# ScalarE's Sigmoid ahead of a nop, a difference behind a product, and a gate product one bundle earlier, in a fused convolution and channel-mix kernel

## The chip, the cores and the metric

The kernel runs on one core of a Trainium2 chip. Time is device time in microseconds (us) for one execution; a run's figure is the median of its executions. The engines of the core work side by side, each through its own queue in order: TensorE (PE in the profile, with PEld for its weight loads), VectorE (DVE), ScalarE (ACT), GpSimd (POOL) and SyncE (SP), of which the last here only issues transfers.

## The reference, cut to what matters

Eight sequences of 4160 rows with 192 columns go through a causal convolution over 7 rows, whose weights are a softmax for each of 8 heads, and then through a channel mix. `*` is elementwise, `@` a matrix product.

```python
# first stage: the convolution, per head h with 24 columns
out[b, s, h, :] = sum_k softmax(weight)[h, k] * x_padded[b, s + k, h, :]

# second stage, x is now the first stage's result
x_prev = x shifted by one row
xk = mu_k * x + (1 - mu_k) * x_prev
xr = mu_r * x + (1 - mu_r) * x_prev
k  = maximum(xk @ w_k, 0)            # 192 -> 1024 columns
v  = k * k @ w_v                     # 1024 -> 192 columns
r  = 1 / (1 + exp(-(xr @ w_r)))      # 192 -> 192 columns
out = r * v
```

## The kernel before

Sequences are worked on in pairs, p = 0 to 3, one in each half of the 128 partitions. A pair is cut into *steps* of 512 rows; the first pair begins and ends with a step of 256, and the last 64 rows of all pairs form one last step. Each step has `ns` slots (8 for 512 rows, 4 for 256): one slot is one tile of k, a product of six matmuls with 1024 results per partition. Four consecutive slots make a *bundle*. Bundles are counted from 0 (b0); step 8 is the second 256-row step of the first pair and fills b15, step 9 is the first of the second pair and fills b16 and b17. R and V are made in *quads* of 256 rows (s, j), one in each bundle, behind their step:

```python
quads = []
vb = 1
for s, (p, t0, L, n0, ns) in enumerate(steps):
    for j in range(L // 256):
        vb = max(vb, last_bundle[s]) + 1
        quads.append((s, j, vb))
```

All results of TensorE lie in one ring of four tiles[...]. k tiles, R tiles, V tiles and convolution tiles all come from it, and a tile's place is free again when the instruction that reads it out is done:

```python
ring = ctx.enter_context(tc.tile_pool(name="ring", bufs=4, space=bass.MemoryType.PSUM))

def k_relu(n):                                   # frees a k tile
    ...
    nc.scalar.activation(out=k_sb, in_=ps.rearrange("p a b -> p (a b)"), func=AF.Relu)

def r(s, j):                                     # twelve matmuls
    xr = xrs[s]
    ps = ring.tile([P, 2, BANK], FP32, tag="k", name="ps_r")
    ...

def r_out(s, j):                                 # frees an R tile
    r_sbs[s, j] = three.tile([P, 2, 2 * D], BF16, tag="r_sb", name="r_sb")
    nc.scalar.activation(out=r_sbs[s, j], in_=r_ps.pop((s, j))[:, :, 0 : 2 * D], func=AF.Sigmoid)

def v_rows(s, j, half, ks=(0, 1)):               # V, thirty-two matmuls in each half
    ...
    if half == 0:
        nc.scalar.clobber_nop([nc.scalar.lower_ap(v_ps[s, j])])

def v_out(s, j):                                 # V's product with R: frees a V tile
    ...
    nc.vector.tensor_tensor(out=..., in0=v_ps.pop((s, j)), in1=r_sbs.pop((s, j)), op=ALU.mult)
```

The nop is an instruction of ScalarE that does nothing. It waits for V's first half and V's second half waits for it, so that the two halves, which use the two row groups of TensorE with the two banks of the tile exchanged, never meet.

VectorE makes the inputs of k and R: a difference of two shifted views of the convolution's result, then `scale` by mu and `add_y` for xk and for xr. xk and xr have two buffers each, taken in turns by the steps:

```python
def diff(s, cs=slice(0, 3)):
    ...
    nc.vector.tensor_tensor(out=..., in0=y_of(s, cs, 1), in1=y_of(s, cs, 0), op=ALU.subtract)

def scale(s, i, *cs, act=False):
    ...
        (xks, xrs)[i][s] = two.tile([P, NC, STEP], BF16, tag=("xk", "xr")[i], name=("xk", "xr")[i])
    ...
```

The convolution of later rows is woven in as *units* of eight matmuls, two units in each of b2 to b5 and then in every odd bundle from b7 to b53; ScalarE copies each unit's tile out. Its result goes to memory and comes back by a transposing transfer (`y_read`), from which `diff` reads. From b3 on, all bundles with k tiles have this form, in the order in which each engine meets its share:

```python
def bundle_rest(b, ns):
    units = xt.get(b, [])
    quad = vq[b][0]
    for n in bundles[b - 1][2 if b == 3 else 3 :]:
        k_square(n)
    run(mix_a, b)
    if b > 3:
        v_out(*vq[b - 1][0])
    k_mm(ns[0])
    k_relu(ns[0])
    k_mm(ns[1])
    k_relu(ns[1])
    run(mix_b, b)
    k_square(ns[0])
    k_square(ns[1])
    run(mix_c, b)
    k_mm(ns[2])
    k_relu(ns[2])
    run(rq, b)            # r
    v_rows(*quad, 0)
    run(rs, b)            # r_out, the Sigmoid
    k_square(ns[2])
    k_mm(ns[3])
    k_relu(ns[3])
    for u in units:
        conv_tiles(*u)
        conv_tiles_out(*u)
    v_rows(*quad, 1)
    run(late, b)
```

What the tables hold of a step s whose first slots are in bundle fb:

```python
            if s == 2:
                at(mix_c, 1, diff, s)
            elif s == 4:
                at(mix_a, fb - 1, diff, s)
            else:
                at(mix_c, fb - 2, diff, s)
            at(mix_a, fb - 1, scale, s, 0, 0)
            at(mix_b, fb - 1, scale, s, 0, 1, 2)
            at(mix_c, fb - 1, add_y, s, 0)
            ...
                at(mix_c, fb - 1, scale, s, 1, 0)
                at(mix_a, fb, scale, s, 1, 1)
            at(mix_b, fb, scale, s, 1, 2)
            at(mix_b, fb, add_y, s, 1)
    ...
    for s, j, vb in quads:
        at(rq, vb - (s == LAST), r, s, j)
        at(rs, vb - (s == LAST), r_out, s, j)
        ...
```

Of the kernel before, what the change touches and what calls it, by code (L numbers as in the profile page):

```python
# [14 lines left out]
def kernel(  # L15
# [56 lines left out]
    T0, LAST = S - TAIL, len(steps) - 1  # L72
# [12 lines left out]
    last_bundle = [bundle_of[st[3] + st[4] - 1] for st in steps]  # L85
# [202 lines left out]
    def conv_tiles(g, c):  # L288

        nb = groups[g][2]  # L290
        if c == 0:
            ys[g] = two.tile([P, GB, 2 * D], BF16, tag="y", name="y")
        ps = ring.tile([P, 2, BANK], FP32, tag="k", name="ps_c")
        conv_ps[g, c] = ps
        m = nb // 2
        banks = ps[:, :, 0 : m * 4 * G].rearrange("p i (m s c) -> p i m s c", m=m, s=2)
        for k in range(2):
            h = 2 * c + k
            for i in range(2):
                q = slice(i * Q, (i + 1) * Q)  # L300
                for j in range(2):
                    nc.tensor.matmul(  # L302
                        out=banks[j * Q : (j + 1) * Q, i, :, :, k * G : (k + 1) * G],
                        lhsT=toe[q, h, q],
                        rhs=xbs[g][q, j * m : (j + 1) * m, :, h * G : (h + 1) * G],
                        start=True,
                        stop=True,
                    )
# [217 lines left out]
    def k_mm(n, cs=range(NC)):  # L526


        s, j = slots[n]
        L = steps[s][2]  # L530
        xk = xks[s]
        if cs[0] == 0 and n not in k_ps:
            k_ps[n] = ring.tile([P, 2, BANK], FP32, tag="k", name="ps_k")
        ps = k_ps[n]
        nf = STEP // L

        for c in cs:
            for f in range(nf):
                fs = slice((j * nf + f) * P, (j * nf + f + 1) * P)
                for i in range(2):  # L540
                    r = slice(i * Q, (i + 1) * Q)
                    nc.tensor.matmul(  # L542
                        out=ps[:, i, f * L : (f + 1) * L],
                        lhsT=wk[r, c, fs],
                        rhs=xk[r, c, :L],
                        start=c == 0 and f == 0,
                        stop=c == NC - 1 and f == nf - 1,
                    )

    def k_relu(n):  # L550
        ps = k_ps.pop(n)
        k_sb = four.tile([P, 2 * STEP], BF16, tag="k_sb", name="k_sb")
        k_sbs[n] = k_sb
        nc.scalar.activation(out=k_sb, in_=ps.rearrange("p a b -> p (a b)"), func=AF.Relu)  # L554

    def k_square(n):
        s, j = slots[n]
        L = steps[s][2]
        k_sb = k_sbs.pop(n)
        if j == 0:  # L560
            k2s[s] = three.tile([P, NF, 2 * STEP], BF16, tag="k2", name="k2")
        nf = STEP // L
        i = k_sb
        o = k2s[s][:, j, :]
        if nf > 1:
            i = k_sb.rearrange("p (b f t) -> p f b t", b=2, f=nf)
            o = k2s[s][:, j * nf : (j + 1) * nf, 0 : 2 * L].rearrange("p f (b t) -> p f b t", b=2)
        nc.vector.tensor_tensor(out=o, in0=i, in1=i, op=ALU.mult)  # L568
# [3 lines left out]
# [4 lines that stand above are left out]
# [44 lines left out]
    def v_rows(s, j, half, ks=(0, 1)):  # L620

        if half == 0:
            v_ps[s, j] = ring.tile([P, 2, BANK], FP32, tag="k", name="ps_v")[:, :, 0 : 2 * D]
        for k in ks:
            for f in range(NF):
                for i in range(2):
                    q = slice(i * Q, (i + 1) * Q)
                    bank = (i + half) % 2
                    t = tile_of(s, j, 2 * bank + k)
                    nc.tensor.matmul(  # L630
                        out=v_ps[s, j][:, bank, k * D : (k + 1) * D],
                        lhsT=k2s[s][q, f, t * P : (t + 1) * P],
                        rhs=wv[q, f, :],
                        start=half == 0 and k == 0 and f == 0,
                        stop=half == 1 and k == 1 and f == NF - 1,
                    )
        if half == 0:
            nc.scalar.clobber_nop([nc.scalar.lower_ap(v_ps[s, j])])

    def tile_of(s, j, k):  # L640
        return k // 2 * (steps[s][2] // P) + 2 * j + k % 2

    def v_out(s, j):
        p, t0, L, _, _ = steps[s]
        o_sb = three.tile([P, 4, D], FP32, tag="o_sb", name="o_sb")
        nc.vector.tensor_tensor(  # L646
            out=o_sb.rearrange("p (b t) d -> p b (t d)", b=2),
            in0=v_ps.pop((s, j)),
            in1=r_sbs.pop((s, j)),
            op=ALU.mult,  # L650
        )
        for st in range(2):
            c = t0 + 2 * j * P
            nc.sync.dma_start(
                out=out[2 * p + st, c : c + 2 * P, :].rearrange("(m p) d -> p m d", p=P),
                in_=o_sb[:, 2 * st : 2 * st + 2, :],
            )
# [24 lines left out]
    early, rq, rs, xt, mix_a, mix_b, mix_c, vq, late = ({} for _ in range(9))  # L682

    def at(table, b, fn, *a):
        table.setdefault(b, []).append((fn, a))
# [7 lines left out]
    for g, (p, base, nb, fb, on_pe) in enumerate(groups):  # L693
# [12 lines left out]
        if g > 4:  # L706

            b = {5: 1, 6: 2, 7: 7}.get(g)
            b = first_bundle[first_step[p]] + (-15, -11, -7, -3)[(g - 6) % 4] if b is None else b
# [3 lines left out]
    for s, (p, t0, L, n0, ns) in enumerate(steps):  # L713
        fb = first_bundle[s]
        if s == 0:
            at(mix_a, 1, mix, s, 1)
            continue
        if s == 1:
            at(mix_b, 1, scale, s, 1, 0, 1)
            at(late, 2, scale, s, 1, 2)  # L720
            at(late, 2, add_y, s, 1)
        else:
            if s == 2:
                at(mix_c, 1, diff, s)
            elif s == 4:
                at(mix_a, fb - 1, diff, s)
            else:
                at(mix_c, fb - 2, diff, s)
            at(mix_a, fb - 1, scale, s, 0, 0)
            at(mix_b, fb - 1, scale, s, 0, 1, 2)  # L730
            at(mix_c, fb - 1, add_y, s, 0)
            if s == 2:
                at(mix_a, fb, scale, s, 1, 0)
                at(mix_b, fb, scale, s, 1, 1)
# [5 lines that stand above are left out]
        if s == LAST - 1 or s < LAST and steps[s + 1][0] > p:  # L740
            at(late, fb - 1, keep_tail, p)
    for s, j, vb in quads:
        at(rq, vb - (s == LAST), r, s, j)
        at(rs, vb - (s == LAST), r_out, s, j)
        if s == LAST:
            at(late, vb, v_last, s, j)
        else:
            vq.setdefault(vb, []).append((s, j))

    def run(table, b):  # L750
        for fn, a in table.get(b, ()):
            fn(*a)
# [114 lines left out]
# [17 lines that stand above are left out]
        k_mm(ns[2])  # L884
        k_relu(ns[2])
        run(rq, b)
        v_rows(*quad, 0)
        run(rs, b)
        k_square(ns[2])
        k_mm(ns[3])  # L890
        k_relu(ns[3])
# [5 lines that stand above are left out]
# [87 lines left out]
```

## Time and profile before

| what | value |
|---|---|
| time, median of 3 | 424.53 us (424.3 to 425.72) |
| span of the profiled execution | 423.4 us, TensorE clock 0.999 of full |
| TensorE busy | 409.8 us (97%) |
| VectorE busy | 371.2 us (88%) |
| ScalarE busy | 354.9 us (84%) |
| V's matmuls, 4032 | 188.2 us |
| k's matmuls, 1632 | 190.8 us |
| R's matmuls, 780 | 43.2 us |
| convolution of later rows, 448 matmuls | 21.6 us |
| Relu of a k tile, 260 | 1032 ns each |
| Sigmoid, 65 | 811 ns each |
| V's product with R, 64 | 953 ns each |
| transfers | 65.58 MB, 155 GB/s in the mean |

Busy times of matmuls overlap, since two row groups of TensorE work side by side, so the shares of the lines add up to more than TensorE's. The clearest measure of pace is the distance from one bundle's R to the next one's: 5.73 us in a bundle without convolution and 6.57 us in one with two units of 240 columns, nearly everywhere from 53 us to the end.

In the lines below, L599 is R's matmuls, L610 the Sigmoid, L630 V's matmuls, L542 k's, L554 the Relu, L568 the square, L302 the convolution, L319 its copies, L480 `diff`, L516 `scale`, L522 `add_y` and L646 V's product. A line of the timeline gives start, length, engine, line, operation, tiles, shapes, count, and in brackets the idle time of the engine before it with what ended that time.

### The profile page before, as it was taken

To read this page: it belongs to the slowest core of one execution; us is meant where nothing else is said; L and a number is where in the kernel's file an instruction comes from. 1 tells how busy PE (TensorE), PEld (TensorE's weight loads), DVE (VectorE), ACT (ScalarE), POOL (GpSimd) and SP (SyncE) were. 2 spreads that over 40 slices of the span, in tenths; PEclk is the share of its full clock that TensorE was granted. 3 is DMA by queue.
4 is the path that set the end of the run, shared out by engine and by line. 5 is a ranking of instruction groups with operands and counts; after the bars stand their busy time and mean duration, and the time that the engine had idled before them with its cause. 6 is when DMAs were issued, how large, how long until landed. Compare 5 with 4: busy or idle time off the path is not lost.

```text
span 423.4 us, 16804 instructions
## 1 busy us (share of the span) xinstructions
PE 409.8 (97%) x7350; PEld 302.7 (71%) x7350; DVE 371.2 (88%) x671; ACT 354.9 (84%) x429; POOL 65.5 (15%) x102
## 2 busy tenths in 40 slices
PE   7899899999979999999999999999999999999996
PEld 5566576777757677677767677776777777777895
DVE  5989799999699889889989988898998889999973
ACT  6899978889768898888889888888898888877781
POOL 8650013012040110304022020302200000000000
PEclk9999999999999999999999999999999999999999
DMA  9999889979649696887859798696972735412223
GB/s 145 175 190 207 177 208 176 221 148 180 166 82 224 143 207 163 123 209 133 199 131 210 197 120 212 96 231 139 180 187 63 194 99 144 119 54 76 77 77 112
DMA packets 137657, 65.58 MB, mean 155 GB/s; under 512 B 87388, under 2 KB 137584, under 8 KB 137584
## 3 DMA queue, kind: packets, MB, share of 16 engines
q1 hardware_dynamic: 95840, 48.42, 43.1%
q0 software_dynamic: 40944, 15.53, 32.3%
q8 instruction: 57, 0.93, 0.9%
q10 hardware_dynamic: 800, 0.57, 0.4%
q14 instruction: 16, 0.13, 0.1%
HBM read 31.62 MB, written 37.09 MB: 162 GB/s over the span
## 4 chain that ended last, share of the span: by engine, by line
PE 86%; DMA 5%; DVE 3%; POOL 2%; issue 1%; ACT 1%; SPq 0%; DVEq 0%; ACTq 0%; POOLq 0%
PE ps_v L630 37%; PE ps_k L542 35%; PE ps_r L599 7%; PE ps_c L302 4%; DMA xb<-in_x_dram 2%; DMA yT<-y_dram 2%; PE ps_v L582 1%; DMA y_dram<-y 1%; POOL xb L136 1%; DVE k L568 1%; DVE o_sb L646 1%; POOL wk L208 1%; DVE xr L522 0%; DVE xr L516 0%; ACT y L319 0%
## 5 line engine op out<-in xcount | busy, mean ns | idle before, releaser
L554 ACT ACTIVATE k_sb<-ps_k 128x1024 bf16<-128x1024 f32 x260 | 252.8, 1032 | 30.5 <-PE ps_k L542 29.0
L568 DVE TENSOR_TENSOR k<-k_sb 128x1024 bf16<-128x1024 bf16 x260 | 173.0, 686 | 32.5 <-ACT k_sb L554 32.0
L542 PE MATMUL ps_k<-xk,wk 64*128 64x512 bf16 (+1 forms) x1632 | 190.8, 367 | 1.7 <-DVE xk L522 0.8
L630 PE MATMUL ps_v<-wv,k 64*128 64x192 bf16 x4032 | 188.2, 243 | 0.3 <-ACT k_sb L554 0.2
L630 PEld LDWEIGHTS <-k 64*128 64x128 bf16 x4032 | 168.0, 94 | 13.7 <-issue 4.5
L542 PEld LDWEIGHTS <-wk 64*128 64x128 bf16 x1632 | 80.4, 94 | 60.0 <-issue 2.1
L610 ACT ACTIVATE r_sb<-ps_r 128x768 bf16<-128x768 f32 x65 | 52.6, 811 | 25.0 <-PE ps_v L630 24.3
L136 POOL DMA_DIRECT2D xb<-in_x_dram x62 | 45.1, 734 | 180.3 <-issue 88.5
L646 DVE TENSOR_TENSOR o_sb<-ps_v,r_sb 128x768 f32<-128x768 f32 x64 | 61.0, 953 | 3.3 <-issue 2.4
L319 ACT CAST y<-ps_c 128x960 bf16<-128x960 f32 (+5 forms) x84 | 51.1, 698 | 0.0
L599 PEld LDWEIGHTS <-xr 64*128 64x128 bf16 x780 | 34.5, 94 | 19.7 <-issue 5.4
L599 PE MATMUL ps_r<-wr,xr 64*128 64x192 bf16 x780 | 43.2, 243 | 4.2 <-DVE o_sb L646 4.1
L516 DVE TENSOR_SCALAR xr<-d,mu 128x512 bf16<-128x512 bf16 (+1 forms) x102 | 35.1, 351 | 4.0 <-PE ps_r L599 4.0
L480 DVE TENSOR_TENSOR d<-yT 128x1536 bf16<-128x1536 bf16 (+3 forms) x37 | 31.4, 852 | 2.7 <-ACT yT L381 1.3
L516 DVE TENSOR_SCALAR xk<-d,mu 128x512 bf16<-128x512 bf16 (+1 forms) x98 | 31.9, 352 | 0.1
L522 DVE TENSOR_TENSOR xr<-xr,yT 128x1536 bf16<-128x1536 bf16 (+1 forms) x33 | 31.0, 939 | 1.1
L522 DVE TENSOR_TENSOR xk<-xk,yT 128x1536 bf16<-128x1536 bf16 (+2 forms) x34 | 30.5, 899 | 0.1
L302 PE MATMUL ps_c<-xb,toe 64*64 64x240 bf16 (+1 forms) x448 | 21.6, 268 | 0.2
L302 PEld LDWEIGHTS <-toe 64*64 64x64 bf16 x448 | 10.4, 105 | 15.9 <-issue 15.9
L464 POOL COPY y_tail<-yT 128x195 bf16<-128x195 bf16 x4 | 3.0, 750 | 65.9 <-DMA yT<-y_dram 65.8
L111 POOL MEMSET xb<- 32x384 bf16 x3 | 1.3, 423 | 43.9 <-DVE xb L109 43.9
L371 PEld LDWEIGHTS <-xb 128*32 128x32 bf16 (+3 forms) x264 | 5.1, 115 | 2.4 <-ACT xb L230 1.4
(59 smaller groups left out, 65.7 us busy)
## 6 DMA issues: line engine op xcount, KB each, us to landing
out_dram<-o_sb SPq DMA_DIRECT2D x128, 192.0 KB
xb<-in_x_dram POOLq DMA_DIRECT2D x40, 240.0 KB, 7.9
y_dram<-y SPq DMA_DIRECT2D x44, 210.0 KB
y_dram<-y SPq DMA_DIRECT2D x12, 168.0 KB
xb<-in_x_dram POOLq DMA_DIRECT2D x10, 192.0 KB, 5.6
xb<-in_x_dram POOLq DMA_DIRECT2D x6, 216.0 KB, 6.7
xb<-in_x_dram POOLq DMA_DIRECT2D x6, 144.0 KB, 5.5
wk<-in_moe_w_k_dram POOLq DMA_DIRECT2D x4, 96.0 KB, 4.7
```

The lines of the kernel that those rows point to most:

```text
L136: nc.gpsimd.dma_start(out=xb[q0 : q0 + rows, lo:hi, s, :], in_=bass.AP(tensor=x.tensor, offset=x.offset + (b * S + t0 + lo * step) * D, ap ...
L302: nc.tensor.matmul(out=banks[j * Q : (j + 1) * Q, i, :, :, k * G : (k + 1) * G], lhsT=toe[q, h, q], rhs=xbs[g][q, j * m : (j + 1) * m, :, ...
L319: nc.scalar.copy(out=bass.AP(tensor=y.tensor, offset=y.offset + d, ap=[y.ap[0], [m * 2 * D, 2], [2 * D, m], [Q, 2], [1, b - a]],), in_=bas ...
L516: nc.vector.tensor_scalar(out=t[:, c, :L], in0=diffs[s][:, c, :L], scalar1=mu[:, i, c : c + 1], scalar2=None, op0=ALU.mult)
L522: nc.vector.tensor_tensor(out=o, in0=o, in1=y_of(s, sl, 0), op=ALU.add)
L542: nc.tensor.matmul(out=ps[:, i, f * L : (f + 1) * L], lhsT=wk[r, c, fs], rhs=xk[r, c, :L], start=c == 0 and f == 0, stop=c == NC - 1 and f ...
L554: nc.scalar.activation(out=k_sb, in_=ps.rearrange("p a b -> p (a b)"), func=AF.Relu)
L568: nc.vector.tensor_tensor(out=o, in0=i, in1=i, op=ALU.mult)
L599: nc.tensor.matmul(out=ps[:, i, k * D : (k + 1) * D], lhsT=xr[q, c, ts], rhs=wr[q, c, :], start=c == 0, stop=c == NC - 1,)
L610: nc.scalar.activation(out=r_sbs[s, j], in_=r_ps.pop((s, j))[:, :, 0 : 2 * D], func=AF.Sigmoid)
L630: nc.tensor.matmul(out=v_ps[s, j][:, bank, k * D : (k + 1) * D], lhsT=k2s[s][q, f, t * P : (t + 1) * P], rhs=wv[q, f, :], start=half == 0 ...
L646: nc.vector.tensor_tensor(out=o_sb.rearrange("p (b t) d -> p b (t d)", b=2), in0=v_ps.pop((s, j)), in1=r_sbs.pop((s, j)), op=ALU.mult,)
```

## The change

It has three parts, all of them a matter of order; no instruction is added and none taken away.

1. In bundles with convolution the Sigmoid comes ahead of the nop in ScalarE's queue, so that it need not wait for V's first half. Bundles without convolution keep the old order.
2. The fifth step's difference (s = 4), and the first `scale` that reads it, move from ahead of V's product to behind it in VectorE's queue. This difference is the first to read what the first transposing transfer brings.
3. R and its Sigmoid are put no later than one bundle (for j = 0) behind their step's last slots, so that R no longer falls back where V does.

```diff
             if s == 2:
                 at(mix_c, 1, diff, s)
             elif s == 4:
-                at(mix_a, fb - 1, diff, s)
+                at(mix_b, fb - 1, diff, s)
             else:
                 at(mix_c, fb - 2, diff, s)
-            at(mix_a, fb - 1, scale, s, 0, 0)
+            at(mix_b if s == 4 else mix_a, fb - 1, scale, s, 0, 0)
             at(mix_b, fb - 1, scale, s, 0, 1, 2)
...
     for s, j, vb in quads:
-        at(rq, vb - (s == LAST), r, s, j)
-        at(rs, vb - (s == LAST), r_out, s, j)
+        b = min(vb, last_bundle[s] + 1 + j) if s else vb
+        at(rq, b, r, s, j)
+        at(rs, b, r_out, s, j)
...
         run(rq, b)
+        if units:
+            run(rs, b)
         v_rows(*quad, 0)
-        run(rs, b)
+        if not units:
+            run(rs, b)
         k_square(ns[2])
```

## Prediction

> **What bounds the kernel now.** I read the page's busy shares first, then a table of busy time over two bundles in mid-kernel (65.35 to 77.64 us, one bundle with convolution and one without).
>
> ```profile
> PE 409.8 (97%) x7350; PEld 302.7 (71%) x7350; DVE 371.2 (88%) x671; ACT 354.9 (84%) x429; POOL 65.5 (15%) x102
> ```
>
> ```profile
> core 0: us, PE busy (x) PEld busy (x) DVE busy (x) ACT busy (x) POOL busy (x), PEclk, DMA share, GB/s
> 65.35:77.64 12.29, 12.29 (x218) 8.92 (x216) 11.34 (x21) 10.84 (x14) 3.58 (x5) 1.00 1.42 195
> ```
>
> TensorE is the bound: busy in all 12.29 us of the pair, at full clock, while VectorE has 0.95 us and ScalarE 1.45 us to spare. So a shorter wait on ScalarE or VectorE is worth something only where TensorE stands behind it. Where that is, the chain of waits says (waiter, releaser, us in total, times, longest):
>
> ```profile
> ACT r_sb L610 <- PE ps_v L630: 24.3, 60, 2.7
> PEld L302 <- issue: 15.9, 55, 0.4
> PE ps_r L599 <- DVE o_sb L646: 4.1, 3, 2.2
> DVE xr L516 <- PE ps_r L599: 4.0, 1, 4.0
> DVE d L480 <- DMA yT<-y_dram: 1.3, 1, 1.3
> ```
>
> The longest wait is the Sigmoid's, 24.3 us, but it is ScalarE that waits. A busy TensorE can also hide a wait, since the ends of pipelined matmuls are modelled. I therefore looked at one bundle with convolution in order of time:
>
> ```profile
> 174.79 0.82 PE L542 MATMUL ps_k<-xk,wk 64*128 64x512 bf16 x6
> 175.08 0.81 ACT L610 ACTIVATE r_sb<-ps_r 128x768 bf16<-128x768 f32 x1 [0.34 <-PE ps_v L630]
> 175.54 0.24 PEld L302 LDWEIGHTS <-toe 64*64 64x64 bf16 x9 [0.42 <-issue]
> 175.54 0.79 PE L302 MATMUL ps_c<-xb,toe 64*64 64x240 bf16 x16
> 175.94 0.14 PEld L302 LDWEIGHTS <-toe 64*64 64x64 bf16 x7 [0.16 <-issue]
> ```
>
> The Sigmoid ends at 175.08 + 0.81 = 175.89; the weight loads of the convolution stop after nine and go on at 175.94. The sixteen matmuls go in sets of four; set 3 is the first of the second tile. In the single records, set 4 follows set 3 by 0.102 us, but set 3 follows set 2 by 0.268. In all 27 bundles of this form set 3 starts 0.051 or 0.052 us after the Sigmoid's end. The cause is the ring: its four slots are handed out in the order in which they come back. In a bundle with convolution V takes the first k tile's slot, the last k tile the second's, the first convolution tile the third's, and the second convolution tile R's, which the Sigmoid empties. TensorE does stand behind the Sigmoid, for 0.166 us a bundle (0.208 where a set streams 192 columns: 0.289 - 0.081).
>
> Two single losses remain. The first, in bundle 6:
>
> ```profile
> 49.56 2.11 PE L542 MATMUL ps_k<-xk,wk 64*128 64x512 bf16 x18
> 53.05 0.67 PE L599 MATMUL ps_r<-wr,xr 64*128 64x192 bf16 x12 [1.38 <-DVE o_sb L646]
> ```
>
> ```profile
> 50.78 0.96 DVE L480 TENSOR_TENSOR d<-yT 128x1536 bf16<-128x1536 bf16 x1 [1.28 <-DMA yT<-y_dram]
> 52.04 0.95 DVE L646 TENSOR_TENSOR o_sb<-ps_v,r_sb 128x768 f32<-128x768 f32 x1
> ```
>
> VectorE waits for a transposing transfer with the fifth step's difference; V's product (o_sb) is queued behind, and R needs the slot that the product empties. The second, in bundles 16 and 17:
>
> ```profile
> 110.54 0.96 DVE L522 TENSOR_TENSOR xk<-xk,yT 128x1536 bf16<-128x1536 bf16 x1
> 115.45 0.35 DVE L516 TENSOR_SCALAR xr<-d,mu 128x512 bf16<-128x512 bf16 x1 [3.96 <-PE ps_r L599]
> 122.86 0.95 DVE L646 TENSOR_TENSOR o_sb<-ps_v,r_sb 128x768 f32<-128x768 f32 x1
> ```
>
> ```profile
> 114.74 0.67 PE L599 MATMUL ps_r<-wr,xr 64*128 64x192 bf16 x12
> 119.54 2.12 PE L542 MATMUL ps_k<-xk,wk 64*128 64x512 bf16 x18
> 123.87 0.67 PE L599 MATMUL ps_r<-wr,xr 64*128 64x192 bf16 x12 [2.21 <-DVE o_sb L646]
> ```
>
> VectorE stands 3.96 us: xr has two buffers, step 9 writes step 7's, and step 7's second R runs only at 114.74, in bundle 16. After that VectorE has no gap until 133.6, and bundle 17's R waits for its late product. From R to R that bundle took 9.13 us; plain ones take 5.73.
>
> **What the Trainium skill says.** "TensorE: Matmul & The Clock Gate", section "Wait — 56ns, not 53.3ns?", gives N / 2.4 GHz + 2.5 ns from start to start, 215.7 ns for 512 columns; the trace has 1.94 us for nine pairs, 0.216: k products are at the floor. "ScalarE: Activation LUTs", section "What ACT_TABLE_LOAD costs", gives 186 ns + 0.833 N and an overlap of some 93 ns between neighbours: 826 ns for 768 columns. The trace has 811 and a successor 0.70 to 0.71 us after the start; it agrees, so a Sigmoid moved in its queue carries 0.71 us with it. "TensorEngine Tiling (Array Packing)", section "Key Properties", says that a change of tiling mode drains the engine. The trace agrees at both edges of the convolution: 0.306 us from the last k pair to set 1 instead of 0.216, and 0.230 from set 4 to V instead of 0.102. The change leaves these. The same page, "Gotcha 1: PSUM Pressure", says that different row tiles can't access one bank at once; no run here tries that, but it is what the nop between V's halves is for.
>
> **Part 1, Sigmoid ahead of the nop.** Nothing is added; one ScalarE instruction changes places. In the bundle shown the relus run from 171.88 to 174.74 (2.86). R ended about 173.6, so the Sigmoid can start at some 174.64 instead of 175.08 and end at 175.45. Set 3, unhindered, is due at 175.54 + 0.127 + 0.102 = 175.77, 0.27 later than the slot then comes back (175.50). The nop follows the Sigmoid, by about 175.4, well ahead of V's second half near 176.1. So the whole 0.166 should go. ScalarE keeps up: the last relu waits for the last k tile, about 0.13 us earlier than now, and the casts follow. VectorE's spare 0.95 us per pair is more than 0.17. Counting: bundle 3 gains nothing, since its Sigmoid already runs straight behind the relus (33.23, no wait). Bundles 4 and 5 would gain 0.34, but bundle 6 then waits for the transfer (part 2), which does not move. Bundles 7, 9, 11, 13, 15: 5 x 0.166 = 0.83. Bundle 17 counts in part 3. Of the eighteen from 138.7 on, twelve stream 240 columns and six 192: 12 x 0.166 + 6 x 0.208 = 3.24. Sum 4.07 us.
>
> **Part 2, the difference behind the product.** VectorE is free at 49.49, V's end is 49.56 plus some 0.2, so the product runs about 49.8 to 50.7 and R needs no wait: it starts at 51.5 instead of 53.05. But the transfer still lands at 50.75, and from there VectorE has one chain: difference 0.99, three scales 0.78, two squares 1.20, addition 0.88, scale 0.27, two squares 1.24, scale 0.27 = 5.63, so bundle 7's own product starts at 56.4 instead of 57.78 and ends at 57.3. Bundle 7's R, at 58.78 now, follows at 57.35: 1.4 us. The 0.34 of bundles 4 and 5 lies inside this, not on top.
>
> **Part 3, R earlier.** The new rule takes the smaller of V's bundle and last bundle + 1 + j. For 512-row steps both agree: step 7, j = 1, stays in bundle 16 (14 + 1 + 1). Only step 8, with 256 rows, moves, from 17 to 16. So the R that VectorE waits 3.96 us for is not moved, and this wait stays. What goes is bundle 17's R and its wait for the product. TensorE can then finish bundle 17 by 126.9 or earlier instead of 128.50, even if the doubled R in bundle 16 makes V wait for the third k tile's slot (its relu ends at 117.52, so V starts there instead of at 115.66). But VectorE's queue is as long as before: bundle 17's product still ends at 129.6, and bundle 18's R waits for it: 129.65 instead of 130.44. Gain 0.8 us. VectorE's first gap before, 0.70 us at 133.6, is about what this uses up.
>
> Sum: 4.07 + 1.4 + 0.8 = 6.3 us; 424.5 - 6.3 = **418.2 us**.
>
> **Rivals.** *The Sigmoid's wait is off the path*: TensorE is 97% busy and ScalarE idles anyway; then parts 2 and 3 alone give 2.2 us, 422.3. For it: the page shows no TensorE wait at L302. Against it: 27 starts at a fixed 0.05 us behind the Sigmoid. *The R move frees everything*: if bundle 17 lost no time, 3.4 us instead of 0.8 would come back, 415.6. Against it: the 3.96 us belong to an R that stays. *The second R costs*: both R tiles of bundle 16 hold slots until V's first half is done, because the plain bundle keeps the Sigmoid behind the nop. If V or the last k tile then waited past VectorE's lag, part 3 would turn into a loss of 1 to 2 us: 420 to 421. *A new wait at set 3*: the next candidate, the relu ahead of the Sigmoid, empties its slot earlier, so I give this little.
>
> **Range and chances.** Part 1 is surest, 3.5 to 4.4; part 2 0.9 to 1.6; part 3 -1 to 1.6. With some 0.7 us between runs (424.3 to 425.72), eight in ten lie in 416.9 to 420.8. Two per cent is 8.5 us, which needs part 3 at its best and more: 0.06. A loss of 2% has no source in the profile: 0.01.
>
> **What would show it.** Right: pairs of bundles take 12.12 us instead of 12.29 (12.05 instead of 12.26 with 192 columns), set 3 comes 0.10 us after set 2, the Sigmoid's wait for V goes in bundles with convolution and stays near 0.33 in the others; bundle 7's R is near 57.35; the 3.96 us wait is still there and the R of bundle 18 follows its product. Wrong: set 3 still late behind another ScalarE instruction; the wait of 3.96 us gone; V or the last k tile of bundle 16 late by more than 2 us.

## The result and the profile after

The changed kernel takes 417.5 us (417.38 to 417.75, four runs) against 424.82 us before on the same chip (424.3 to 425.72). The ratio is 0.9826, 95% interval 0.9808 to 0.9845: 7.3 us less, 1.7%. The prediction was 418.2 us, range 416.9 to 420.8.

The busy shares of the kernel after, from the page, and then the busy table of one pair of bundles, 62.97 to 75.07 us (bundles 8 and 9, from R to R, the pair shown of before):

```profile
PE 404.4 (97%) x7349; PEld 301.3 (72%) x7350; DVE 369.5 (89%) x671; ACT 354.9 (85%) x429; POOL 65.2 (16%) x102
```

```profile
core 0: us, PE busy (x) PEld busy (x) DVE busy (x) ACT busy (x) POOL busy (x), PEclk, DMA share, GB/s
62.97:75.07 12.10, 12.10 (x218) 8.90 (x216) 11.34 (x21) 10.84 (x15) 3.58 (x5) 1.00 1.43 216
```

VectorE and ScalarE do the same work to the hundredth, 11.34 and 10.84 us; TensorE "is busy" 0.19 us less, with the same matmuls. So 0.19 us of its busy time before was no work: the modelled ends of the matmuls covered it. The page's 97% says the same before and after; only the length of the pair tells.

The chain of waits after (waiter, releaser, us in total, times, longest):

```profile
ACT r_sb L610 <- PE ps_v L630: 11.3, 35, 1.7
PEld L302 <- issue: 10.8, 27, 0.4
DVE xr L516 <- PE ps_r L599: 3.8, 1, 3.8
PE ps_v L630 <- ACT k_sb L554: 1.4, 2, 1.2
```

The Sigmoid's wait for V is left in 35 bundles, those without convolution. The weight loads of the convolution stop 29 times instead of 55 (27 in the line above, two more put down to the Sigmoid): once ahead of each of the 28 convolutions, and once inside that of bundle 3. VectorE's wait for R of step 7 is still there. V's wait for a Relu has grown from 0.2 us to 1.4.

**Part 1**, one bundle with convolution in order of time:

```profile
170.19 0.83 ACT L610 ACTIVATE r_sb<-ps_r 128x768 bf16<-128x768 f32 x1
170.37 0.83 PE L542 MATMUL ps_k<-xk,wk 64*128 64x512 bf16 x6
171.13 0.35 PEld L302 LDWEIGHTS <-toe 64*64 64x64 bf16 x16 [0.42 <-issue]
171.13 0.60 PE L302 MATMUL ps_c<-xb,toe 64*64 64x240 bf16 x16
171.66 0.86 PEld L630 LDWEIGHTS <-k 64*128 64x128 bf16 x22 [0.18 <-issue]
```

The Sigmoid ends at 171.02, before the convolution starts; its sixteen weight loads go through in one piece, and the sixteen matmuls span 0.60 us instead of 0.79. In the single records set 3 follows set 2 by 0.102 us (0.268 before), as set 4 follows set 3. One thing more than expected: V follows set 4 by 0.205 us instead of 0.230. Bundles with convolution take 6.38 us instead of 6.57, and 6.30 instead of 6.53 with 192 columns.

**Part 2**, VectorE and then TensorE in bundles 5 to 7:

```profile
48.54 0.96 DVE L646 TENSOR_TENSOR o_sb<-ps_v,r_sb 128x768 f32<-128x768 f32 x1 [0.21 <-PE ps_v L630]
49.99 0.96 DVE L480 TENSOR_TENSOR d<-yT 128x1536 bf16<-128x1536 bf16 x1 [0.49 <-DMA yT<-y_dram]
55.58 0.95 DVE L646 TENSOR_TENSOR o_sb<-ps_v,r_sb 128x768 f32<-128x768 f32 x1
```

```profile
48.33 2.11 PE L542 MATMUL ps_k<-xk,wk 64*128 64x512 bf16 x18
50.27 0.66 PE L599 MATMUL ps_r<-wr,xr 64*128 64x192 bf16 x12
56.59 0.67 PE L599 MATMUL ps_r<-wr,xr 64*128 64x192 bf16 x12 [0.43 <-DVE o_sb L646]
```

The product now runs while VectorE would wait for the transfer, and R of bundle 6 starts without a wait. R of bundle 7 still waits 0.43 us for its product, as VectorE's chain from the transfer's landing said. From the start of that difference to R of bundle 7 it is 8.00 us before and 6.60 after.

**Part 3**, TensorE, one Relu of ScalarE, and VectorE in bundles 16 to 18:

```profile
111.67 0.67 PE L599 MATMUL ps_r<-wr,xr 64*128 64x192 bf16 x12
112.58 0.67 PE L599 MATMUL ps_r<-wr,xr 64*128 64x192 bf16 x12 [0.25 <-ACT k_sb L554]
114.50 1.50 PE L630 MATMUL ps_v<-wv,k 64*128 64x192 bf16 x32 [1.24 <-ACT k_sb L554]
120.79 1.50 PE L630 MATMUL ps_v<-wv,k 64*128 64x192 bf16 x32 [0.89 <-DVE o_sb L646]
126.68 0.66 PE L599 MATMUL ps_r<-wr,xr 64*128 64x192 bf16 x12
```

```profile
113.42 1.02 ACT L554 ACTIVATE k_sb<-ps_k 128x1024 bf16<-128x1024 f32 x1 [0.89 <-DVE k L568]
```

```profile
112.38 0.35 DVE L516 TENSOR_SCALAR xr<-d,mu 128x512 bf16<-128x512 bf16 x1 [3.83 <-PE ps_r L599]
119.79 0.95 DVE L646 TENSOR_TENSOR o_sb<-ps_v,r_sb 128x768 f32<-128x768 f32 x1
125.38 0.95 DVE L646 TENSOR_TENSOR o_sb<-ps_v,r_sb 128x768 f32<-128x768 f32 x1
```

Bundle 16 has two Rs. VectorE still stands 3.83 us. The late product of bundle 16 (119.79) now holds V of bundle 17, not R. From the first R of bundle 16 to the R of bundle 18 it is 15.01 us, before 9.13 + 6.57 = 15.70.

Where the 7.7 us between the two profiled spans (423.4 and 415.7) come from, by distances of starts:

| stretch | before | after | gain | predicted |
|---|---|---|---|---|
| start to the fifth step's difference | 50.78 | 49.99 | 0.79 | 0 |
| that difference to R of b7 (part 2) | 8.00 | 6.60 | 1.40 | 1.4 |
| R of b7 to R of b16 (part 1) | 55.96 | 55.08 | 0.88 | 0.83 |
| R of b16 to R of b18 (part 3, and part 1 in b17) | 15.70 | 15.01 | 0.69 | 0.8 |
| R of b18 to the last R (part 1) | 282.81 | 279.14 | 3.67 | 3.24 |
| last R to the end | 10.14 | 9.92 | 0.22 | 0 |

The first and the last row are no gain of the change. The fifth step's difference starts when a transfer lands, and in the eight kernels e1 to e8 below it starts anywhere from 50.08 to 50.69, with and without each part. Here the whole lead is there before the first instruction that changes its place: R of bundle 3 starts at 30.98 us before and at 30.18 after. In the last row TensorE's work is equally long, 6.06 us from the last R to the end of the last matmul; the 0.22 us lie behind it. The three parts make 6.64 us.

### The profile page after: what moved, and what is told of

Read it like the earlier page. It is cut to its first block, busy times and chain, and to the rows that moved or that the text cites. A ratio compares the mean times of both kernels' runs of the same rounds, so it can differ in the third digit from the quotient of the medians.

```text
span 415.7 us, 16804 instructions
## 1 busy us (share of the span) xinstructions
PE 404.4 (97%) x7349; PEld 301.3 (72%) x7350; DVE 369.5 (89%) x671; ACT 354.9 (85%) x429; POOL 65.2 (16%) x102
## 4 chain that ended last, share of the span: by engine, by line
PE 85%; DMA 5%; DVE 3%; ACT 2%; POOL 2%; issue 1%; SPq 0%; ACTq 0%; DVEq 0%; POOLq 0%
PE ps_v L630 38%; PE ps_k L542 35%; PE ps_r L599 7%; PE ps_c L302 3%; DMA xb<-in_x_dram 2%; DMA yT<-y_dram 2%; PE ps_v L582 1%; DMA y_dram<-y 1%; DVE k L568 1%; POOL xb L136 1%; ACT k_sb L554 1%; POOL wk L208 1%; ACT y L319 1%; DVE o_sb L646 1%; DMA out_dram<-o_sb 1%
## 5 line engine op out<-in xcount | busy, mean ns | idle before, releaser
L610 ACT ACTIVATE r_sb<-ps_r 128x768 bf16<-128x768 f32 x65 | 53.2, 821 | 12.0 <-PE ps_v L630 11.3
L302 PE MATMUL ps_c<-xb,toe 64*64 64x240 bf16 (+1 forms) x448 | 16.6, 265 | 0.1
```

Source lines behind the costliest of these rows:

```text
L302: nc.tensor.matmul(out=banks[j * Q : (j + 1) * Q, i, :, :, k * G : (k + 1) * G], lhsT=toe[q, h, q], rhs=xbs[g][q, j * m : (j + 1) * m, :, ...
```

## The experiments

Each stands against the kernel before on the same chip (median 425.2 to 425.8 us in the three sessions). "Theory" is the account held before that run.

**e1, e2, e3: each part alone.** The edits are the three pieces of the change's diff, one at a time.

> Part 1 alone. Theory (the second convolution tile waits for the slot that the Sigmoid empties): set 3 follows set 2 by 0.10 us in all bundles with convolution but b3, bundles 6.38 us (240 columns) or 6.30 (192) instead of 6.57 and 6.53. Gain 18 bundles 3.7, b7 to b15 0.95, b17 0.2, b4 and b5 nothing because b6 then waits longer for the transfer: 4.8 us, 420.0. Rival (the Sigmoid's wait is off TensorE's path): 424.8 as before.

> Part 2 alone. Theory (V's product is freed from behind the transfer, but VectorE's chain from the transfer's landing stays): R of b6 starts 1.5 us earlier, R of b7 1.4 earlier, and 1.4 us is what is left at the end: 423.4. Rival (the next wait for the transfer takes it all back): 424.8.

> Part 3 alone. Theory (the long wait for R of step 7 stays; the late product of b16 now holds V of b17 instead of R): VectorE's wait stays near 3.9 us, gain 0.6 to 0.8 us: 424.1. Rival 1 (the freed R gives back the whole loss of b16 and b17): 3.4 us, 421.4. Rival 2 (the second R tile in b16 costs): 425 or more.

| kernel | time, us | ratio to before, 95% interval | difference to R of b7 | R of b16 to R of b18 |
|---|---|---|---|---|
| e1, part 1 | 419.99 | 0.9875 (0.9849 to 0.9901) | 8.00 | 15.51 |
| e2, part 2 | 423.61 | 0.9965 (0.9951 to 0.9979) | 6.60 | 15.69 |
| e3, part 3 | 423.59 | 0.9958 (0.9943 to 0.9974) | 8.01 | 15.01 |

e1 meets its number: bundles with convolution take 6.38 and 6.30 us, and the rival (off TensorE's path) is out. In e1 bundles 4 and 5 are shorter as well, yet the distance from the transfer's landing to R of b7 stays 8.00: what they save, bundle 6 waits longer. e2 gives its 1.40 us in the trace, to the hundredth, so the next transfer does not take it back. e3 keeps VectorE's wait (3.96 us) and gains 0.69 us from b16 to b18, 0.19 of it because the convolution in b17 no longer has an R slot to wait for. Neither rival (3.4 us, or a loss) came true. Its timed runs show more, 1.8 us with an interval of 1.1 to 2.4; but all nine had a granted TensorE clock of 0.998 of full or more, while 12 of the 25 runs of the kernel before had 0.995 or 0.996 and took 426.06 us in the median, the other 13 424.82, so that 1.2 us are left at equal clock. The 0.5 us beyond the trace lie within the spread of one kernel's runs (those 13: 424.19 to 425.18 us).

**e4: the Sigmoid ahead of the nop everywhere.** The change keeps the old order in bundles without convolution. Is that needed?

```diff
         run(rq, b)
-        if units:
-            run(rs, b)
+        run(rs, b)
         v_rows(*quad, 0)
-        if not units:
-            run(rs, b)
```

> The kernel after, with the Sigmoid ahead of the nop in bundles without convolution too. Theory (there V's second half follows the last k tile at once and waits for the nop, which now comes behind the Sigmoid): in plain bundles that follow one with convolution the relus end about 0.6 us before the second half is due, the Sigmoid then ends 0.1 us too late, so each of some 24 such bundles is 0.1 to 0.25 us longer: 420 to 423. Rival (the order matters to convolution alone, ScalarE has time enough): 417.5 as after.

Measured: 417.24 us, ratio 0.9804 (0.9781 to 0.9826), the same as the kernel after. The theory fell. ScalarE and TensorE in a plain bundle that follows one with convolution:

```profile
260.99 0.89 ACT L610 ACTIVATE r_sb<-ps_r 128x768 bf16<-128x768 f32 x1
```

```profile
259.80 1.48 PE L630 MATMUL ps_v<-wv,k 64*128 64x192 bf16 x32
261.12 0.81 PE L542 MATMUL ps_k<-xk,wk 64*128 64x512 bf16 x6
261.77 0.41 PE L630 MATMUL ps_v<-wv,k 64*128 64x192 bf16 x6
```

V's second half starts at 261.77, 0.11 us before the Sigmoid ends (261.88), although the nop that it waits for stands behind the Sigmoid. In the records the nop is a semaphore instruction of ScalarE's sequencer, not of the engine: it starts at 260.02 and ends at 261.33, when V's first half is done, with the Sigmoid still running. It passes while an earlier instruction computes. In the kernel after it does so in bundles with convolution too: in the one shown, the nop ends at 170.59 and the Sigmoid at 171.02. So the queue's order holds for the work of ScalarE's engine, not for this nop. The Trainium skill, "Perfetto Trace Analysis", section "Sequencer Loop", has engine instructions pushed into a queue and control instructions carried out by the sequencer itself; the trace agrees. So the order costs nothing either way in plain bundles (5.72 to 5.73 us in both kernels), and the condition in the change is not needed for time.

**e5: the Sigmoid behind the last Relu**, in bundles with convolution, in the kernel before.

```diff
         v_rows(*quad, 0)
-        run(rs, b)
+        if not units:
+            run(rs, b)
         k_square(ns[2])
         k_mm(ns[3])
         k_relu(ns[3])
+        if units:
+            run(rs, b)
         for u in units:
```

> The kernel before, with the Sigmoid behind the last Relu in bundles with convolution. Theory (set 3 waits for the Sigmoid's slot): set 3 again starts 0.05 us after the Sigmoid's end, now some 1.5 us later than in the kernel before; about 25 bundles longer by 1 to 1.5 us: 450 to 462. Rival (set 3 is late because of the change of tiling or the weight loads): set 3 stays 0.27 us behind set 2 and the time within 1% of 424.8.

Measured: 444.6 us, ratio 1.045 (1.0404 to 1.0495). Neither number: the bundles are 0.79 us longer (7.36 from R to R), not 1 to 1.5.

```profile
170.82 0.40 PE L302 MATMUL ps_c<-xb,toe 64*64 64x240 bf16 x8
170.93 1.02 ACT L554 ACTIVATE k_sb<-ps_k 128x1024 bf16<-128x1024 f32 x1 [0.91 <-PE ps_k L542]
171.85 0.80 ACT L610 ACTIVATE r_sb<-ps_r 128x768 bf16<-128x768 f32 x1
172.01 0.40 PE L302 MATMUL ps_c<-xb,toe 64*64 64x240 bf16 x8 [0.78 <-ACT k_sb L554]
```

Set 3 starts at 172.01, behind the last Relu (170.93 + 1.02 = 171.95), not behind the Sigmoid (172.65). So with a late Sigmoid the second convolution tile took the last k tile's place in the ring and no longer R's. The edit moved the cause along with the effect and does not tell the Sigmoid's part; e9 does it with the slots kept.

**e9 and e10: the Sigmoid done twice**, in bundles with convolution, the first time into a tile that nothing reads; once in the kernel before, once in the kernel after. All slots stay where they were. The edit in the kernel before:

```diff
+    spare = const.tile([P, 2, 2 * D], BF16)
+
+    def twice(b):
+        for _, (s, j) in rs.get(b, ()):
+            nc.scalar.activation(out=spare, in_=r_ps[s, j][:, :, 0 : 2 * D], func=AF.Sigmoid)
...
         v_rows(*quad, 0)
+        if units:
+            twice(b)
         run(rs, b)
```

> The kernel before, with the Sigmoid done twice in bundles with convolution, the first time into a tile that nothing reads; the order of slots is that of before. Theory: the slot comes back 0.71 us later, and set 3 still starts 0.05 us after the second Sigmoid's end: 0.98 us behind set 2, 0.71 us for each of some 26 bundles, 18.5 us, 443 to 444. Rival (set 3 is late because of the change of tiling or the weight loads): set 3 stays at 0.27 behind set 2 and the time within 1% of before.

> The kernel after, with the same second Sigmoid. Theory: in the kernel after the slot is back 0.33 us before set 3 starts, 0.28 more than the 0.05 it needs, so of the added 0.71 us only some 0.43 reach TensorE: set 3 about 0.53 us behind set 2, some 24 bundles x 0.43 = 10.3 us, 428. Rival: as above, 417.5.

Measured: e9 442.92 us, ratio 1.0421 (1.0376 to 1.0466); e10 428.74 us, ratio 1.0091 (1.0061 to 1.0121); both are near what the theory gave, and the rival (no change) is out. In e9, ScalarE and TensorE:

```profile
182.42 0.81 ACT L616 ACTIVATE spare<-ps_r 128x768 bf16<-128x768 f32 x1 [0.34 <-PE ps_v L636]
183.12 0.81 ACT L610 ACTIVATE r_sb<-ps_r 128x768 bf16<-128x768 f32 x1
```

```profile
182.88 0.40 PE L302 MATMUL ps_c<-xb,toe 64*64 64x240 bf16 x8
183.98 0.40 PE L302 MATMUL ps_c<-xb,toe 64*64 64x240 bf16 x8 [0.70 <-ACT r_sb L610]
```

Set 3 comes 0.97 us behind set 2 and 0.05 behind the second Sigmoid's end (183.12 + 0.81 = 183.93). The wait is now long enough that the profile itself names it: PE waits for r_sb, L610. In e10 TensorE:

```profile
175.88 0.40 PE L302 MATMUL ps_c<-xb,toe 64*64 64x240 bf16 x8
176.53 0.40 PE L302 MATMUL ps_c<-xb,toe 64*64 64x240 bf16 x8 [0.25 <-ACT r_sb L610]
```

Here set 3 comes 0.53 us behind set 2, as expected: of the 0.71 us added, 0.28 vanish in the slack that the change made. This shows the cause of part 1 and measures its margin. The 0.230 us from set 4 to V are back in both, so this longer step goes with a convolution that was stopped between its tiles.

**e6: parts 1 and 2 without part 3.**

> Parts 1 and 2 without part 3. Theory (gains add, but b4 and b5 of part 1 count only inside part 2): 6.3 to 6.7 us, 418.2. Rival (part 3 gives nothing once part 1 is there): 417.5 as after.

Measured: 418.31 us, ratio 0.984 (0.9812 to 0.9868), not to be told from the kernel after (0.9808 to 0.9845). In the traces b16 to b18 take 15.51 us here and 15.01 after: part 3 is worth 0.5 us on top of part 1.

**e7 and e8: a third buffer for xr**, e7 with parts 1 and 2, e8 with the whole change.

```diff
-            (xks, xrs)[i][s] = two.tile([P, NC, STEP], BF16, tag=("xk", "xr")[i], name=("xk", "xr")[i])
+            (xks, xrs)[i][s] = (two, three)[i].tile([P, NC, STEP], BF16, tag=("xk", "xr")[i], name=("xk", "xr")[i])
```

> Parts 1 and 2, no part 3, and a third buffer for xr, so that step 9 need not wait for step 7's second R. Theory (that wait is the cause of the loss in b16 and b17): VectorE's wait of 3.8 us is gone, b16 to b18 take 5.73 + 6.38 = 12.1 us instead of 15.0, 414.6. Rival (VectorE is behind there in any case, at the change of pairs): the lag comes back as another wait, 417 to 418.

> The kernel after with a third buffer for xr. Theory: the wait of 3.8 us is gone as without part 3, but the two R tiles of b16 make V wait about 1 us for the third k tile's Relu, so part 3 now costs: 415.2 to 415.8, slower than the version without it. Rival (the early R is good in itself): equal or faster than the version without part 3, 414.6 or less.

Measured: e7 415.14 us, ratio 0.9758 (0.9731 to 0.9785); e8 415.99 us, ratio 0.9784 (0.9756 to 0.9812). VectorE at the place of the long wait, and TensorE's Rs of b16, b17 and b18, both in e7:

```profile
108.30 0.95 DVE L522 TENSOR_TENSOR xk<-xk,yT 128x1536 bf16<-128x1536 bf16 x1
109.17 0.35 DVE L516 TENSOR_SCALAR xr<-d,mu 128x512 bf16<-128x512 bf16 x1
```

```profile
112.30 0.66 PE L599 MATMUL ps_r<-wr,xr 64*128 64x192 bf16 x12
118.03 0.67 PE L599 MATMUL ps_r<-wr,xr 64*128 64x192 bf16 x12
124.41 0.66 PE L599 MATMUL ps_r<-wr,xr 64*128 64x192 bf16 x12
```

The wait is gone and b16 to b18 take 12.11 us, 5.73 + 6.38, the pace of any other pair, where e6 takes 15.51 and the kernel after 15.01. The wait was the cause of the whole 3.4 us, and e7 is faster than the kernel before by 10.7 us in the medians (9.2 at equal clock) and, by its interval, faster than the kernel after. With the wait gone part 3 costs: in e8 the same stretch takes 12.82 us. Not for the reason expected, though. VectorE and TensorE of e8:

```profile
116.75 0.69 DVE L568 TENSOR_TENSOR k<-k_sb 128x1024 bf16<-128x1024 bf16 x1 [1.57 <-ACT k_sb L554]
117.62 0.95 DVE L646 TENSOR_TENSOR o_sb<-ps_v,r_sb 128x768 f32<-128x768 f32 x1
```

```profile
111.68 1.15 PE L599 MATMUL ps_r<-wr,xr 64*128 64x192 bf16 x24
112.68 1.50 PE L630 MATMUL ps_v<-wv,k 64*128 64x192 bf16 x32
118.62 1.50 PE L630 MATMUL ps_v<-wv,k 64*128 64x192 bf16 x32 [0.54 <-DVE o_sb L646]
```

V of b16 follows the two Rs at once. The two Sigmoids of b16 (114.28 to 115.79) stand ahead of its last Relu, which comes late, so VectorE waits 1.57 us for it, the product comes late, and V of b17 waits for that. Part 3 is a remedy for a stall, and one that needs the stall. The whole runs of e7 and e8 do not separate (their intervals overlap); the 0.71 us is that of the traces.

## Why the prediction was right, point by point

*Part 1* was right in place, cause and count (e1, e9, e10). Mis-sized was one term: 0.166 us a bundle (0.208 with 192 columns) became 0.191 and 0.23, because the step from set 4 to V also shrank, by 0.025; the prediction had said of both edges of the convolution that "the change leaves these". Over the 23 bundles counted this makes some 0.5 us (bundle 15 gave only 0.12), and with it the sum of 4.07 us became 4.55. That bundles 4 and 5 would count for nothing, because bundle 6 waits for the transfer, held: 8.00 us in e1. So did bundle 3: after the change its set 3 is still 0.336 us behind set 2.

The step on the nop, that it "follows the Sigmoid" in time, was wrong (e4, and the kernel after itself): it passes ahead of the Sigmoid's end. It did no harm, since the second half was due later in any case.

*Part 2* was right: 1.40 us, from VectorE's chain behind the landing, and R of b7 still behind its product.

*Part 3* was right in what it does not do: the wait on step 7's R stays (3.83 us), V of b16 waits for the third k tile's Relu (it starts at 114.50, the Relu ends at 113.42 + 1.02 = 114.44), and most of the loss stays. The size, 0.69 us instead of 0.8, is near. But the step that gave it failed: "bundle 18's R waits for" the product of bundle 17. That R starts at 126.68, 0.35 us after the product's end, without a wait. What holds TensorE is the same late queue of VectorE one product earlier: V of b17 waits 0.89 us for the product that empties b16's V tile, so it lies in that tile's slot. The prediction had V take a slot that a Relu empties, an order carried over from other bundles; with one more R tile in b16 it was another. That the size came out near is in part luck.

Of the rest of the profiled spans, 0.79 us is a lead that was there ahead of the change, and 0.22 lies behind TensorE's last matmul. So the prediction's 6.3 us stand against 6.64 for the change in the traces, and 7.3 in the timed runs.

Of the rivals, "off the path" and "frees everything" are out by e1 and e3. "The second R costs" is out in the kernel after but true in e8. "A new wait at set 3" is out: set 3 follows set 2 by 0.10 us in every bundle with convolution but b3, which the prediction had left out.

## What to carry to other kernels

An engine shown as 97% busy can be waiting inside that: compare distances between starts of equal work, and look for starts that follow another engine's end by a constant (here 0.05 us in 27 bundles of 27). A wait that is long in the table is worth only what stands behind it in the ring: here 24 us of Sigmoid waits hid less than 5. Before moving work away from a stall, ask what the stalled engine waits for: one more buffer gave 3.4 us in two bundles where the reordering gave 0.5.

## What was not expected of the hardware

- A nop in ScalarE's queue passes when its semaphores allow, while the activation ahead of it still runs: V, which waits for the nop, started 0.11 us before that activation's end (e4).
- A stop between the two convolution tiles costs more than itself: the step to the next V matmul is 0.230 us with it and 0.205 without (0.210 and 0.185 with 192 columns), in every bundle with convolution of before and after. Why is open.
